# A retention and two-MoE kernel: the first stage reordered, with the weight conversion kept off GpSimd

## The chip, the cores and the metric

The kernel runs on one core of one Trainium2 chip. Its engines are called here as the profile calls them: PE (TensorE, matmuls), DVE (VectorE), ACT (ScalarE), POOL (GpSimd), SP (SyncE, which issues the DMAs). The metric is the device time of one execution in microseconds (us), the median of several runs; lower is better.

## The reference

Three operations follow each other on 3072 tokens (4 batches of 768) with 512 features:

```python
# retention: 8 heads of 64, a decaying state per head
for t in range(S):
    state = gamma[None, :, None, None] * state + np.einsum('bhd,bhe->bhde', k[:, :, t], v[:, :, t])
    y[:, :, t] = scale * np.einsum('bhd,bhde->bhe', q[:, :, t], state)
x = y.transpose(0, 2, 1, 3).reshape(3072, 512)
# first MoE, in fact one dense MLP; w_in is 512x2048, w_out 2048x512
r = np.maximum(x @ w_in, 0.0)
x = (s * (r * r) + b) @ w_out
# second MoE: 8 experts, each token goes to one of them by its sorted gate logits, 384 tokens per expert
logits = x @ w_gate
...
out[mask] = np.maximum(x[mask] @ w1[e], 0.0) @ w2[e]
```

The assignment of tokens follows the order of the logits, so the logits have to be nearly exact, and the kernel works with pairs of numbers: each operand of a large matmul is split into a high part in the type fp32r and the remainder, and three matmuls (high by high, high by low, low by high) stand for one.

## The kernel before, in words

The work is cut into 12 blocks of 256 tokens (0 to 11). Three blocks are one batch, and the retention state runs through them. A block goes through retention, `attn(blk, ...)`, which is four groups (two chunks of 128 tokens, two pairs of heads each), and then through the first MoE, which has 16 slices f of 128 hidden features.

A retention group has two parts. `b_part` issues 8 score matmuls (L330) and 4 mask multiplications on DVE into `am` (L334). `c_part` issues the state update (L347), the products of `am` with v (L353) and those of the state with q (L357), then the copy of the result to `xh` on ACT (L366) and the remainder `xl` on DVE (L367), and after every second group two state scalings on DVE (L373). `scale_chunk` multiplies the next chunk's q and v by decays on POOL (L197, L199). With `wide` the next group's `b_part` stands ahead of this group's `c_part`, with more banks and buffers; without it the parts alternate.

An MoE slice is an H unit and an X unit. `h_unit(blk, f, ...)` issues 12 matmuls of 256 columns (L417), ACT takes the relu into `r` (L420), DVE squares it by a product with the bank (L421); then `r_split` makes the high part `rh` on ACT (L425) and the remainder `rl` on POOL (L426). `x_unit(blk, f, ...)` issues 6 matmuls of 512 columns (L437) that need this pair. After slice 15 `x_out` copies two banks to SBUF on ACT (L447).

The 32 weight tiles (weight 2f is slice f of w_in, weight 2f+1 that of w_out) come as 64-bit words and are converted by `conv_gen`. Per weight: a square on ACT (L235), five operations on DVE (L258, L262, L265, L271, L275), then the high part on ACT (L245) and, on POOL, a subtraction (L247) and an addition (L249), after which the weight is in `READY`. Weights 20 to 31 use the memory of the first six chunks of q, k and v.

The logits of a chunk are eight products with a sum each on DVE (`gate`, L460, one for each expert). `logits_gen` waits for a chunk's result and meanwhile works on rows that depend on weights alone (`const_row`).

The order in which instructions are issued is written out at build time; nothing is moved afterwards. A `Side` is a generator that yields planned nanoseconds, a `Weave` issues units of PE work of planned cost and steps each side whose planned time has come. Each engine then runs its own queue in that order and waits by semaphores. In the first stage (lines 557 to 581):

- retention of blocks 0, 1 and 2 (wide), with conversion steps in between until weight 2 is ready;
- then `moe1((0, 1, 2), ...)`: for each f the H units of blocks 0, 1, 2, the X units two units behind; conversion goes on in between;
- after the last weight chunks 6 and 7 and the gate weights are loaded, and retention of block 3 (wide) runs alone;
- then the logits side is added, and the MoE of blocks 3, 4, ... follows, each woven with the next block's retention.

Of the kernel before, what the change touches and what calls it, by code (L numbers as in the profile page):

```python
# [20 lines left out]
F32 = mybir.dt.float32  # L21
# [60 lines left out]
def kernel(  # L82
# [16 lines left out]
    PRO=1.5,  # L99
    PN=2,  # L100
    CY=(560, 890),
# [4 lines left out]
    DV=(0, 2),  # L106
    WARM=24,
    XP=(1, 1),
# [120 lines left out]
    def conv_gen():  # L229
# [22 lines left out]
        for n in range(2 * NF):  # L252
# [13 lines left out]
            if last:  # L266
                parts(1)
            if n + 1 < 2 * NF:
                square(n + 1)
            yield CY[1]  # L270
            DVE.tensor_scalar(p.bitcast(I32), ai, -0x800000, None, op0=OP.bitwise_and)  # L271
            yield CY[0]
            if last:
                parts(2)
            DVE.scalar_tensor_tensor(p, lo32, 2.0 ** -52, p, op0=OP.mult, op1=OP.mult)  # L275
# [133 lines left out]
    def h_unit(blk, f, hb):  # L409
# [11 lines left out]
        DVE.scalar_tensor_tensor(r, ph, 0.0, r, op0=OP.max, op1=OP.mult)  # L421
# [41 lines left out]
    def logits_gen():  # L463


        for c in range(NC - 4):
# [51 lines left out]
    def conv_until(n):  # L518
        while n not in READY:
            conv.step()  # L520

    def moe1(blks, xbs, lag, apart=0):


        units = []
        seq = [(f, i) for f in range(NF - apart) for i in range(len(blks))]
        seq += [(f, i) for i in range(len(blks)) for f in range(NF - apart, NF)]
        for n in range(len(seq) + lag):
            if n < len(seq):
                def hu(n=n):  # L530
                    f, i = seq[n]
                    conv_until(2 * f + 1)
                    r = h_unit(blks[i], f, 2 + n % 2)
                    rhl = work.tile([128, 2, TB], F32R, name="rhl", bufs=3)
                    R2[blks[i], f] = r_split(r, rhl[:, 0], rhl[:, 1],
                                             DVE if len(blks) > 1 and n % DV[1] < DV[0] else POOL)
                units.append((1320, hu))
            if n >= lag:
                def xu(n=n - lag):
                    f, i = seq[n]  # L540
                    x_unit(blks[i], f, xbs[i])
                    if f == NF - 1:
                        x_out(blks[i])
                units.append((1300, xu))
        return units
# [11 lines left out]
    def attn3():  # L557
        for b in range(3):
            yield from attn(b, True)

    a3 = Side(attn3())
    conv.due = 3000.0
    while not a3.done:
        if conv.due < a3.due and PN not in READY:
            t = conv.due
            conv.step()
# [21 lines left out]
    for blk in range(3, NB - 2):  # L588
        nxt = Side(attn(blk + 1, False) if blk < NB - 3 else attn2())
        wv.add(nxt)  # L590
        units = moe1((blk,), ((0, 1),), 2)
# [549 lines left out]
```

## Time and profile before

| what | value |
|---|---|
| median of 3 runs | 1154.41 us (1153.56 to 1155.1) |
| profiled execution | 1160.23 us, span of its instructions 1158.5 us |
| PE busy, share of the span | 1044.8 us, 90% |
| DVE busy | 788.0 us, 68% |
| POOL busy | 581.7 us, 50% |
| ACT busy | 349.2 us, 30% |

The profiled execution is 5.8 us above the median; all sums below are made within the profiled execution. The trace gives the times of its instructions from the start of the span. The landmarks of the first stage are: first conversion instruction at 11.5 us, end of the retention of blocks 0 to 2 at 50.8 us, last weight ready at 219.9 us, retention of block 3 from 232.9 us, first MoE matmul of block 3 at 243.9 us.

### The profile page before, as it was taken

The page shows a single profiled execution, that of the slowest core. Times are in us where ns is not written, and L with a number is a line of the kernel's source. Part 1 is how long each engine was busy: PE and PEld are TensorE (multiplying, and loading weights), DVE is VectorE, ACT ScalarE, POOL GpSimd, SP SyncE. Part 2 cuts the span into 40 slices and gives each one's busy share as a digit, 9 for nine tenths or more (in the row PEclk, how much of TensorE's full clock was granted, in tenths as well). Part 3 has the DMA queues.
Part 4 walks back from the last instruction along what each step waited for, and adds up shares of the span by engine and source line. Part 5 has one row for each costly group of instructions (what it writes and reads, how often), then busy time and mean ns, then how long its engine had stood idle before and what let it go on. Part 6 is the DMA issues. An engine that isn't in the chain of part 4 may idle for free. (4 is left out here: it accounts for less than half of the span.)

```text
span 1158.5 us, 19641 instructions
## 1 busy us (share of the span) xinstructions
PE 1044.8 (90%) x7526; PEld 889.8 (77%) x7526; DVE 788.0 (68%) x1889; ACT 349.2 (30%) x776; POOL 581.7 (50%) x543
## 2 busy tenths in 40 slices
PE   6888777899999999999999999958988978989997
PEld 5766666788887878887888898747877767778996
DVE  5899999579979988979855533556667576572210
ACT  1333333322322222222222342123233333335511
POOL 4377777642355545464523342045354664648811
PEclk8999999999999999999999999978989989899999
DMA  9223222232120202021111000243243343426400
GB/s 322 90 91 91 92 91 91 71 103 74 55 82 20 73 10 71 23 81 36 58 46 47 25 1 1 81 130 119 84 137 119 119 133 106 145 81 201 137 28 28
DMA packets 31727, 98.29 MB, mean 85 GB/s; under 512 B 4496, under 2 KB 4880, under 8 KB 31632
## 3 DMA queue, kind: packets, MB, share of 16 engines
q1 hardware_dynamic: 27216, 83.40, 22.9%
q0 software_dynamic: 3840, 12.59, 3.2%
q8 instruction: 59, 0.97, 0.3%
q10 hardware_dynamic: 576, 1.05, 0.2%
q14 instruction: 36, 0.29, 0.1%
HBM read 84.43 MB, written 12.58 MB: 84 GB/s over the span
## 5 line engine op out<-in xcount | busy, mean ns | idle before, releaser
L460 DVE SCALAR_TENSOR_TENSOR scr<-tmp,wg 128x512 bf16<-128x512 f32 x288 | 260.5, 904 | 27.6 <-POOL tmp L485 22.4
L426 POOL TENSOR_TENSOR rhl<-r,rhl 128x256 fp32r<-128x256 f32 x160 | 133.8, 836 | 278.9 <-ACT rhl L425 220.3
L437 PE MATMUL b<-h,rhl 128*128 128x512 f32 x640 | 229.9, 402 | 3.6 <-ACT rhl L425 2.1
L954 POOL TENSOR_TENSOR l<-eraw,h 128x512 fp32r<-128x512 f32 x128 | 161.2, 1288 | 140.2 <-ACT h L953 114.9
L417 PE MATMUL b<-xh,h 128*128 128x256 f32 x704 | 204.9, 291 | 28.3 <-DVE r L421 26.9
L417 PE MATMUL b<-xh,l 128*128 128x256 f32 x704 | 199.6, 283 | 0.0
L417 PE MATMUL b<-xl,h 128*128 128x256 f32 x704 | 199.5, 283 | 0.0
L417 PEld LDWEIGHTS b<-xh,h 128*128 128x128 f32 x704 | 134.8, 192 | 45.5 <-DVE r L421 36.9
L437 PEld LDWEIGHTS b<-h,rhl 128*128 128x128 f32 x640 | 121.4, 191 | 32.2 <-ACT rhl L425 4.5
L417 PEld LDWEIGHTS b<-xl,h 128*128 128x128 f32 x704 | 135.0, 192 | 3.7
L417 PEld LDWEIGHTS b<-xh,l 128*128 128x128 f32 x704 | 134.9, 192 | 0.1
L425 ACT ACTIVATE rhl<-r 128x256 fp32r<-128x256 f32 x160 | 66.9, 418 | 224.4 <-DVE r L421 224.4
L421 DVE SCALAR_TENSOR_TENSOR r<-b,r 128x256 f32<-128x256 f32 x192 | 80.5, 419 | 79.3 <-ACT r L420 78.4
L437 PE MATMUL b<-l,rhl 128*128 128x512 f32 x320 | 127.4, 398 | 0.0
L420 ACT ACTIVATE r<-b 128x256 f32<-128x256 f32 x192 | 72.8, 379 | 175.1 <-PE b L417 166.4
L980 PE MATMUL b<-gh,h 128*128 128x384 f32 x256 | 95.4, 373 | 5.3 <-DVE hl L989 5.3
L980 PE MATMUL b<-gl,h 128*128 128x384 f32 x256 | 89.1, 348 | 0.0
L980 PE MATMUL b<-gh,l 128*128 128x384 f32 x256 | 89.0, 348 | 0.0
L983 ACT ACTIVATE hh<-b 128x384 fp32r<-128x384 f32 x64 | 31.5, 492 | 169.0 <-PE b L980 143.4
L1003 PE MATMUL b<-h,hh 128*128 128x512 f32 x192 | 81.6, 425 | 0.0
L1003 PE MATMUL b<-h,hl 128*128 128x512 f32 x192 | 78.0, 406 | 3.9 <-DVE hl L989 3.9
L989 DVE SCALAR_TENSOR_TENSOR hl<-b,hh 128x384 fp32r<-128x384 f32 x64 | 35.3, 552 | 67.0 <-ACT hh L983 64.5
(184 smaller groups left out, 1975.8 us busy)
## 6 DMA issues: line engine op xcount, KB each, us to landing
eraw<-in_w_dram SPq DMA_DIRECT2D x64, 512.0 KB, 3.7
q<-in_qkv_dram SPq DMA_DIRECT2D x36, 512.0 KB, 4.6
raw<-in_w_dram SPq DMA_DIRECT2D x32, 512.0 KB, 3.6
first<-in_qkv_dram SPq DMA_DIRECT2D x24, 256.0 KB, 6.0
x2d<-tmp SPq DMA_DIRECT2D x20, 256.0 KB, 5.7
wg<-in_wgT_dram SPq DMA_DIRECT2D x4, 512.0 KB, 3.8
x2d<-tmp ACTq DMA_DIRECT2D x4, 256.0 KB, 3.7
xg<-x2d,idx POOLq DMA_INDIRECT x24
```

What stands on the lines that cost most here:

```text
L417: PE.matmul(ph, a[:, ks], b[:, kc, :], start=(n == 0), stop=(n == 3 * KC - 1))
L420: ACT.activation(r, ph, AF.Relu)
L421: DVE.scalar_tensor_tensor(r, ph, 0.0, r, op0=OP.max, op1=OP.mult)
L425: ACT.activation(rh, r, AF.Copy)
L426: eng.tensor_tensor(rl, r, rh.bitcast(F32), op=OP.subtract)
L437: PE.matmul(X2[blk][t], a[:, ts], b, start=(f == 0 and i == 0), stop=(f == NF - 1 and i == 2))
L460: DVE.scalar_tensor_tensor(scr, x, 1.0, WG[e], op0=OP.mult, op1=OP.mult, accum_out=of[:, e:e + 1])
L954: POOL.tensor_tensor(lo, raw[:, a, :], hi.bitcast(F32), op=OP.subtract)
L980: PE.matmul(PH[0], a[:, ks], b[:, kc, :], start=(kc == 0 and n == 0), stop=(kc == KC - 1 and n == 2))
L983: ACT.activation(hh, PH[0], AF.Relu)
L989: DVE.scalar_tensor_tensor(hl, ph, 0.0, hh.bitcast(F32), op0=OP.max, op1=OP.subtract)
L1003: PE.matmul(Y[i, t], a[:, ts], b, start=(f == 0 and j == 0), stop=(f == NF2 - 1 and j == 2))
```

## The change

The two POOL operations of the conversion (L247, L249) go to DVE. For blocks 0 to 2 the square of an H unit goes from DVE to ACT (a new `act` argument of `h_unit`) and the remainder of `r_split` from POOL to DVE. In those blocks POOL keeps only `scale_chunk`.

The order of the first stage is written anew. Retention of block 0 is woven with conversion alone. Then conversion and the retention of blocks 1 and 2 are two sides (the retention not wide, planned at 0.45 of its usual pace); as soon as the two weights of a slice are ready, the H unit of block 0 for it is issued, with its X unit. Once the retention of blocks 1 and 2 has been issued, those two blocks are served first, each time the one that has done fewer slices, and block 0 takes slices when neither of them has a weight. X units follow three H units behind, or at once if no H unit can be issued. Chunks 6 and 7 are loaded when the conversion has been issued to its end. When blocks 1 and 2 are finished, the retention of block 3 (not wide) and the logits are added as sides, so that products of the gate stand between the parts of that retention. The planned costs of conversion steps change from (560, 890) to (500, 800), with two more yields for each weight.

```diff
-    CY=(560, 890),
+    CY=(500, 800),
+    SPACE=0.45,
...
             elif step == 1:
-                POOL.tensor_tensor(a, a, W[n][0].bitcast(F32), op=OP.subtract)
+                DVE.tensor_tensor(a, a, W[n][0].bitcast(F32), op=OP.subtract)
             else:
-                POOL.tensor_tensor(W[n][1], a, p, op=OP.add)
+                DVE.tensor_tensor(W[n][1], a, p, op=OP.add)
                 READY.add(n)
...
-        DVE.scalar_tensor_tensor(r, ph, 0.0, r, op0=OP.max, op1=OP.mult)
+        if act:
+            ACT.activation(r, r, AF.Square)
+        else:
+            DVE.scalar_tensor_tensor(r, ph, 0.0, r, op0=OP.max, op1=OP.mult)
         return r
...
-        for c in range(NC - 4):
+        for c in (2, 3, 4, 5, 0, 1, *range(6, NC - 4)):
...
-    a3 = Side(attn3())
+    a0 = Side(attn(0, True))
     conv.due = 3000.0
-    while not a3.done:
-        if conv.due < a3.due and PN not in READY:
-            t = conv.due
-            conv.step()
-            conv.due = t + PRO * (conv.due - t)
+    while not a0.done:
+        min((conv, a0), key=lambda x: x.due).step()
+
+    def attn12():
+        for b in (1, 2):
+            yield from attn(b, False, SPACE)
+
+    a12 = Side(attn12(), a0.due)
+    wv = Weave([conv, a12])
...
+    def h_first(b, f, hb):
+        R2[b, f] = split_to_work(h_unit(b, f, hb, True), DVE)
+        pend.append((b, f))
...
+    while len(OUT) < 3:
+        if conv.done and CPB not in QKV:
+            load_chunk(CPB)
+            load_chunk(CPB + 1)
+            scale_chunk(CPB)
+        if a4 is None and {1, 2} <= OUT:
+            load_gate()
+            a4 = Side(attn(3, False, SPACE), wv.t)
+            wv.add(a4)
+            tail = Side(logits_gen(), wv.t)
+            wv.add(tail)
+        can = [b for b in ((1, 2) if a12.done else ()) + (0,) if at[b] < NF and 2 * at[b] + 1 in READY]
+        can = can[:1] if 0 in can[:1] else sorted((b for b in can if b), key=lambda b: at[b])
+        if len(pend) > 2 or (pend and not can):
+            wv.unit(1300, x_first)
+        elif can:
+            b = can[0]
+            wv.unit(1320, lambda: h_first(b, at[b], 2 + nh % 2))
+            at[b] += 1
+            nh += 1
         else:
-            a3.step()
-    conv.due = 0.0
-    wv = Weave([conv])
-    for u in moe1((0, 1, 2), ((4, 5), (6, 7), (0, 1)), 2):
-        wv.unit(*u)
-    conv_until(2 * NF - 1)
-    load_chunk(CPB)
-    load_chunk(CPB + 1)
-    scale_chunk(CPB)
-    load_gate()
-    a4 = Side(attn(3, True), wv.t)
-    wv.add(a4)
+            s = min((s for s in wv.sides if not s.done), key=lambda s: s.due)
+            wv.t = max(wv.t, s.due)
+            s.step()
     wv.until(lambda: a4.done)
-    tail = Side(logits_gen())
-    wv.add(tail)
```

Three places on DVE show what is moved. Line numbers of the changed kernel differ: L255, L259, L262, L269, L274 are its five conversion operations, L244 and L246 the two that came from POOL, L428 the remainder of an H unit, L423 the square of the later blocks, L333 `am`, L366 `xl`, L372 the state scaling, L462 the gate.

In the middle of the conversion the queue of before has the five operations of a weight, with the squares of H units (L421) among them:

```order
L258 TENSOR_SCALAR tmp<-raw 128x512
L262 SCALAR_TENSOR_TENSOR tmp<-raw,tmp 128x512
L265 SCALAR_TENSOR_TENSOR tmp<-tmp 128x512
L421 SCALAR_TENSOR_TENSOR r<-b_1856,r 128x256
L271 TENSOR_SCALAR tmp<-tmp 128x512
L275 SCALAR_TENSOR_TENSOR tmp<-raw,tmp 128x512
```

The changed kernel has seven there, and remainders (L428) among them:

```order
L255 TENSOR_SCALAR tmp<-raw 128x512
L259 SCALAR_TENSOR_TENSOR tmp<-raw,tmp 128x512
L428 TENSOR_TENSOR rhl<-r,rhl 128x256
L262 SCALAR_TENSOR_TENSOR tmp<-tmp 128x512
L244 TENSOR_TENSOR tmp<-tmp,h_1822 128x512
L269 TENSOR_SCALAR tmp<-tmp 128x512
L246 TENSOR_TENSOR l_1823<-tmp 128x512
L274 SCALAR_TENSOR_TENSOR tmp<-raw,tmp 128x512
```

Both subtractions and additions of a weight now share the queue with the operations on the next weight.

In the retention of block 1 the queue of before holds the `am` of two groups, one conversion step between them, and one more ahead of the first group's `xl`:

```order
L334 SCALAR_TENSOR_TENSOR am<-b_311,mask 128x128
L334 SCALAR_TENSOR_TENSOR am<-b_312,mask 128x128
L334 SCALAR_TENSOR_TENSOR am<-b_311,mask 128x128
L334 SCALAR_TENSOR_TENSOR am<-b_312,mask 128x128
L265 SCALAR_TENSOR_TENSOR tmp<-tmp 128x512
L334 SCALAR_TENSOR_TENSOR am<-b_326,mask 128x128
L334 SCALAR_TENSOR_TENSOR am<-b_327,mask 128x128
L334 SCALAR_TENSOR_TENSOR am<-b_326,mask 128x128
L334 SCALAR_TENSOR_TENSOR am<-b_327,mask 128x128
L271 TENSOR_SCALAR tmp<-tmp 128x512
L367 SCALAR_TENSOR_TENSOR xl<-b_339,xh 128x2x128
```

In the changed kernel the second group of block 1 has the first MoE unit between its two parts (PE runs scores, H unit of block 0, X unit of block 0, then the group's second part):

```order
L333 SCALAR_TENSOR_TENSOR am<-b_353,mask 128x128
L333 SCALAR_TENSOR_TENSOR am<-b_354,mask 128x128
L333 SCALAR_TENSOR_TENSOR am<-b_353,mask 128x128
L333 SCALAR_TENSOR_TENSOR am<-b_354,mask 128x128
L246 TENSOR_TENSOR l_331<-tmp 128x512
L428 TENSOR_TENSOR rhl<-r,rhl 128x256
L274 SCALAR_TENSOR_TENSOR tmp<-raw,tmp 128x512
L366 SCALAR_TENSOR_TENSOR xl<-b_396,xh 128x2x128
L372 TENSOR_TENSOR sbd<-b_195,sdec 64x4x64 x2
```

The remainder of that H unit stands ahead of the group's `xl`. This arrangement occurs in two of the eight groups of blocks 1 and 2.

In the retention of block 3 the queue of before holds nothing but that retention:

```order
L334 SCALAR_TENSOR_TENSOR am<-b_2217,mask 128x128
L334 SCALAR_TENSOR_TENSOR am<-b_2218,mask 128x128
L334 SCALAR_TENSOR_TENSOR am<-b_2217,mask 128x128
L334 SCALAR_TENSOR_TENSOR am<-b_2218,mask 128x128
L367 SCALAR_TENSOR_TENSOR xl<-b_2229,xh 128x2x128
L373 TENSOR_TENSOR sbd<-b_2182,sdec 64x4x64 x2
```

In the changed kernel gate products stand between its parts:

```order
L333 SCALAR_TENSOR_TENSOR am<-b_2216,mask 128x128
L333 SCALAR_TENSOR_TENSOR am<-b_2217,mask 128x128
L333 SCALAR_TENSOR_TENSOR am<-b_2216,mask 128x128
L333 SCALAR_TENSOR_TENSOR am<-b_2217,mask 128x128
L462 SCALAR_TENSOR_TENSOR scr,L<-tmp,wg 128x512 x2
L366 SCALAR_TENSOR_TENSOR xl<-b_2232,xh 128x2x128
L372 TENSOR_TENSOR sbd<-b_2172,sdec 64x4x64 x2
L462 SCALAR_TENSOR_TENSOR scr,L<-tmp,wg 128x512 x2
```

Sixteen of them stand ahead of that block's last `xl`.

## Rows read from the trace of the kernel before

**Rows 1.** Windows: PE, PEld, DVE, ACT, POOL busy (x instructions), clock, DMA share, GB/s

```profile
11.00:50.00 39.00, 31.25 (x244) 24.73 (x244) 31.79 (x81) 8.39 (x20) 20.34 (x16) 0.82 0.68 240
60.00:216.00 156.00, 120.29 (x709) 99.50 (x709) 151.60 (x173) 56.85 (x132) 121.61 (x94) 0.99 0.29 91
...
233.00:244.00 11.00, 9.56 (x97) 7.54 (x97) 5.95 (x23) 2.25 (x6) 4.85 (x5) 1.00 0.35 103
244.00:600.00 356.00, 347.20 (x2369) 300.68 (x2370) 305.46 (x770) 94.65 (x239) 167.04 (x158) 0.99 0.17 51
```

**Rows 2.** Waits of PE from 11 to 244 us: total, times, longest

```profile
PE b L417 <- DVE r L421: 35.7, 30, 2.5
```

**Rows 3.** Timeline of DVE: start, duration, line, operation, tiles

```profile
109.85 0.42 DVE L421 SCALAR_TENSOR_TENSOR r<-b,r 128x256 f32<-128x256 f32 x1
110.18 0.68 DVE L275 SCALAR_TENSOR_TENSOR tmp<-raw,tmp 128x512 f32<-128x512 uint32 x1
110.78 0.42 DVE L258 TENSOR_SCALAR tmp<-raw 128x512 int32<-128x512 int32 x1
111.23 1.11 DVE L262 SCALAR_TENSOR_TENSOR tmp<-raw,tmp 128x512 int32<-128x512 int32 x1
...
204.41 1.66 DVE L262 SCALAR_TENSOR_TENSOR tmp<-raw,tmp 128x512 int32<-128x512 int32 x1
```

**Rows 4.** Timeline of POOL around the same moments, idle time before in brackets

```profile
107.19 1.73 POOL L247 TENSOR_TENSOR tmp<-tmp,h 128x512 f32<-128x512 f32 x1
110.79 1.00 POOL L426 TENSOR_TENSOR rhl<-r,rhl 128x256 fp32r<-128x256 f32 x1 [1.88 <-ACT rhl L425]
...
204.05 1.48 POOL L249 TENSOR_TENSOR l<-tmp 128x512 fp32r<-128x512 f32 x1
```

**Rows 5.** Timeline of DVE, a product of two SBUF tiles of 512 columns

```profile
6.28 0.69 DVE L197 TENSOR_TENSOR first<-first,qdec 128x512 f32<-128x512 f32 x1
```

**Rows 6.** Timeline of DVE, L258 of weights 0, 4, 8 and 31

```profile
11.52 1.37 DVE L258 TENSOR_SCALAR tmp<-raw 128x512 int32<-128x512 int32 x1
...
50.71 0.42 DVE L258 TENSOR_SCALAR tmp<-raw 128x512 int32<-128x512 int32 x1
...
75.69 1.52 DVE L258 TENSOR_SCALAR tmp<-raw 128x512 int32<-128x512 int32 x1
...
209.92 1.17 DVE L258 TENSOR_SCALAR tmp<-raw 128x512 int32<-128x512 int32 x1
```

**Rows 7.** Timeline of PE, first matmul of an H, its X and the next H

```profile
224.44 0.28 PE L417 MATMUL b<-xh,h 128*128 128x256 f32 x1
...
225.88 0.40 PE L437 MATMUL b<-h,rhl 128*128 128x512 f32 x1
...
227.26 0.28 PE L417 MATMUL b<-xhs,h 128*128 128x256 f32 x1
```

**Rows 8.** Timeline of ACT, relu and high part of H units

```profile
111.14 0.36 ACT L420 ACTIVATE r<-b 128x256 f32<-128x256 f32 x1
112.71 0.42 ACT L425 ACTIVATE rhl<-r 128x256 fp32r<-128x256 f32 x1 [1.21 <-DVE r L421]
```

**Rows 9.** Timeline, one retention group: its `am` on DVE, its copy on ACT

```profile
41.67 0.89 DVE L334 SCALAR_TENSOR_TENSOR am<-b,mask 128x128 f32<-128x128 f32 x4
...
43.72 0.38 ACT L366 ACTIVATE xhs<-b 128x256 fp32r<-128x256 f32 x1 [3.16 <-PE b L357]
```

**Rows 10.** Timeline, end of the stage: last weight (POOL), retention and MoE of block 3 (PE)

```profile
218.58 1.29 POOL L249 TENSOR_TENSOR l<-tmp 128x512 fp32r<-128x512 f32 x1
232.89 1.58 PE L330 MATMUL b<-q 64*128 64x128 f32 x16
243.90 0.39 PE L417 MATMUL b<-xh,h 128*128 128x256 f32 x1 [0.29 <-DVE xl L367]
```

**Rows 11.** Timeline of DVE, a gate product with POOL idle

```profile
249.34 0.68 DVE L460 SCALAR_TENSOR_TENSOR scr<-tmp,wg 128x512 bf16<-128x512 f32 x1
...
250.06 1.17 DVE L460 SCALAR_TENSOR_TENSOR scr<-tmp,wg 128x512 bf16<-128x512 f32 x1
```

More of the change, by code (lines that the diff above doesn't have):

```diff
@@ L105 @@
     FZ=(8390, 160),
-    DV=(0, 2),
     WARM=24,
-    XP=(1, 1),
     AG=2,
@@ L265, in conv_gen @@
             DVE.scalar_tensor_tensor(a, p, TINY_WORD * TINY_WORD, a, op0=OP.is_ge, op1=OP.mult)
-            if last:
-                parts(1)
             if n + 1 < 2 * NF:
@@ L270, in conv_gen @@
             yield CY[1]
+            if last:
+                parts(1)
+                yield CY[1]
             DVE.tensor_scalar(p.bitcast(I32), ai, -0x800000, None, op0=OP.bitwise_and)
@@ L274, in conv_gen @@
                 parts(2)
+                yield CY[1]
             DVE.scalar_tensor_tensor(p, lo32, 2.0 ** -52, p, op0=OP.mult, op1=OP.mult)
@@ L407, in split_last, with h_unit @@
             DVE.tensor_tensor(xl[:, ps], XF[i], xh[:, ps].bitcast(F32), op=OP.subtract)
-    def h_unit(blk, f, hb):
+    def h_unit(blk, f, hb, act=False):
         xh, xl = XT[blk]
@@ L516, in const_end, with split_to_work, moe1, hu @@
         ACT.activation(csum[:, 0:E], pc[:, 0:E], AF.Copy)
-    def conv_until(n):
-        while n not in READY:
-            conv.step()
-    def moe1(blks, xbs, lag, apart=0):
+    def split_to_work(r, eng):
+        rhl = work.tile([128, 2, TB], F32R, name="rhl", bufs=3)
+        return r_split(r, rhl[:, 0], rhl[:, 1], eng)
+    def moe1(blk, xb, lag):
         units = []
[L526 to L536, printed above, removed]
+        for n in range(NF + lag):
+            if n < NF:
+                def hu(f=n):
+                    R2[blk, f] = split_to_work(h_unit(blk, f, 2 + f % 2), POOL)
                 units.append((1320, hu))
             if n >= lag:
-                def xu(n=n - lag):
-                    f, i = seq[n]
-                    x_unit(blks[i], f, xbs[i])
+                def xu(f=n - lag):
+                    x_unit(blk, f, xb)
                     if f == NF - 1:
-                        x_out(blks[i])
+                        x_out(blk)
                 units.append((1300, xu))
@@ L555 @@
     scale_chunk(0, DVE)
-    def attn3():
-        for b in range(3):
-            yield from attn(b, True)
-    a3 = Side(attn3())
+    a0 = Side(attn(0, True))
     conv.due = 3000.0
-    while not a3.done:
-        if conv.due < a3.due and PN not in READY:
-            t = conv.due
-            conv.step()
-            conv.due = t + PRO * (conv.due - t)
-        else:
-            a3.step()
-    conv.due = 0.0
-    wv = Weave([conv])
-    for u in moe1((0, 1, 2), ((4, 5), (6, 7), (0, 1)), 2):
-        wv.unit(*u)
@@ L574 @@
-    conv_until(2 * NF - 1)
-    load_chunk(CPB)
-    load_chunk(CPB + 1)
-    scale_chunk(CPB)
-    load_gate()
-    a4 = Side(attn(3, True), wv.t)
-    wv.add(a4)
+    while not a0.done:
[5 more added lines that the diff above has]
+    wv = Weave([conv, a12])
+    wv.t = a0.due
+    XBS = {0: (0, 1), 1: (4, 5), 2: (6, 7)}
+    at = {0: 0, 1: 0, 2: 0}
+    pend = []
@@ new lines, with x_first @@
+    a4 = None
+    nh = 0
+    def h_first(b, f, hb):
+        R2[b, f] = split_to_work(h_unit(b, f, hb, True), DVE)
+        pend.append((b, f))
+    def x_first():
+        b, f = pend.pop(0)
+        x_unit(b, f, XBS[b])
+        if f == NF - 1:
+            x_out(b)
+            OUT.add(b)
+    OUT = set()
+    while len(OUT) < 3:
[18 more added lines that the diff above has]
+            nh += 1
+        else:
+            s = min((s for s in wv.sides if not s.done), key=lambda s: s.due)
+            wv.t = max(wv.t, s.due)
+            s.step()
@@ L590 @@
         wv.add(nxt)
-        units = moe1((blk,), ((0, 1),), 2)
+        units = moe1(blk, (0, 1), 2)
         for i, u in enumerate(units):
```

2 lines of the change are left out of this document (removed).

## The prediction, made before the changed kernel ran

> **What bounds the kernel now.** I read the windows first, because the kernel has stages with different limits. From 244 to 600 us (MoE of the later blocks) PE is busy 347.2 of 356 us [rows 1]: PE is the limit there and 8.8 us are idle. From 60 to 216 us, the conversion of the weights with the MoE of blocks 0 to 2, PE is busy 120.3 of 156 us, DVE 151.6 (97%) and POOL 121.6 [rows 1]: DVE is the limit. The waits of PE agree: 35.7 us of its idle time up to 244 us end with the square on DVE that an H unit needs [rows 2]. So I looked at what occupies DVE. L258 of weight 8 starts at 75.69 and that of weight 31 at 209.92 [rows 6]: 134.2 / 23 = 5.84 us for a weight. A conversion operation on 512 columns takes 0.68 us (L275) or 0.42 (L258), and the same kind of operation also 1.11 or 1.66 us [rows 3]. The difference is POOL: at 110.2 us, where L275 takes 0.68, POOL has ended its L247 at 108.9 and starts again at 110.79; the L262 of 204.41, with 1.66, lies beside the L249 of 204.05 [rows 4]. L421, which reads a PSUM bank, has 0.42 even so. After the last weight (219.9) PE has 13 us of MoE left; at 232.9 the retention of block 3 starts, alone, and the first H unit of block 3 at 243.9 [rows 10]. In those 11 us DVE and PE pass work to and fro (6.0 and 9.6 us busy [rows 1]).
>
> **The change, part by part.** The first stage ends for this sum where H of block 3 starts, 243.9 us now.
>
> 1. Conversion on DVE with POOL idle. The starts in [rows 3] are 0.33 us apart behind L421 (duration 0.42), 0.60 behind L275 (0.68), 0.45 behind L258, whose result the next one needs. So a three-operand operation costs 0.60 to 0.71 and a two-operand one 0.34 to 0.45. The two operations from POOL are of the kind of L197, 0.69 us for 512 columns [rows 5], 0.61 in a chain; this price rests on one row, and its bounds are 0.42 and 0.71. A weight is then 0.45 + 0.71 + 0.60 + 0.61 + 0.34 + 0.61 + 0.60 = 3.9 us (3.5 to 4.3) against 5.84 now. The remainder of an H unit, 256 columns, has no row; half of L197 and L421 bound it at 0.35 and 0.42, in a chain 0.34.
>
> 2. Retention of blocks 0 to 2. Now this and the conversion of weights 0 to 3 take from 11.52 to 50.71 us [rows 6], 39.2 us. Up to the start of weight 8 the changed order has on DVE four weights more (15.6), the two moved operations of the first four (4 x 1.22 = 4.9) and three remainders (1.0). The conversion beside POOL goes: three weights' pairs on POOL of some 1.5 us each stretch DVE now by about half their time, -4 (0 to -7; POOL keeps the scaling of the chunks). Six groups without `wide` wait some 0.5 us for `xl`, since the chain from the end of `am` (42.56) to the end of the copy (44.10) is 1.54 us [rows 9] and some 1.1 us of conversion stand in between: +3. In two groups an H and an X unit stand between the scores and the second part. An H unit is 1.44 us on PE and an X unit 1.38 [rows 7]; relu and high part on ACT are 0.36 and 0.42 [rows 8], the square, which ACT does not do on such a tile now, lies between those, 1.3 us together with the hand-overs. So `xl` comes 1.44 + 1.3 + 0.4 + 1.38 + 0.6 (state update) + 1.54 = 6.7 us after the scores, while DVE has 2.5 us of work: 4.2 us idle, twice, and 1 us at the third early unit, +9.4. Sum: 39.2 + 21.5 - 4 + 3 + 9.4 = 69.1; weight 8 starts at 80.6, and I take 82 because the clock of these 39 us is 0.82 and not 1 [rows 1]. Bounds: 78 (half of the waits) and 93 (PE at 1.2 GHz throughout, below). That is later than now (75.7): this step loses 6 us.
>
> 3. MoE of blocks 0 to 2 from there. PE has 45 H and 44 X units until retention of block 3: 45 x 1.44 + 44 x 1.38 = 125.5 us. DVE has 24 weights x 3.9 + 45 remainders x 0.34 = 109 us. So the limit changes from DVE to PE. DVE queues the remainders among the conversion steps and may have to wait for PE there, and PE for DVE elsewhere; I take 3 us for that (0 to 10), since blocks 1, 2 and 0 alternate and X units come three units behind. PE ends the second part of block 2's last group 1.5 us before weight 8, so the MoE units end at 80.5 + 125.5 + 3 = 209, against 232.9 now.
>
> 4. Retention of block 3. Now 11.0 us. Sixteen gate products come into its DVE queue; a product takes 0.72 us from start to start with POOL idle [rows 11]. Those between `am` and `xl` are hidden by the 1.54 us chain; eight others are not: 5.8 us. One X unit of block 0 adds 1.4. The scaling of chunks on POOL beside gate products (1.17 instead of 0.68 [rows 11]) and the groups without `wide` add some 3. Sum 21 us (17 to 27): H of block 3 starts at 230, 13.9 us earlier than now. So the retention of block 3 isn't hidden; the gate work takes its cover away.
>
> 5. Behind it. The sixteen products are not to be done later, and DVE, busy 305 of 356 us there, holds PE a little less. All PE could gain is its 8.8 us of idle time [rows 1]; most PE time there passes without a wait, so I take 1.5 (0 to 5). The loads: chunks 6 and 7 are issued behind the last weight's load and arrive during the MoE units; the gate weights wait for two staging tiles that are freed with the last weight, beside 4 us of MoE work. If that cover fails, the first gate products hold `xl` of block 3 by 2 to 3 us. The search and the experts behind are not touched. I cost ACT at nothing: a square more for each of 48 units is 0.4 us beside 2.8 us of PE for that unit.
>
> Sum in the profiled execution: 1160.2 - 13.9 - 1.5 = 1144.8 us. That execution is 5.8 us above the median of the runs, so the median of the changed kernel comes to 1139 us.
>
> **A rule weighed against it.** In the retention PE has less to do for a microsecond than now, since the same groups are spread over 70 us with three MoE units. The granted clock of that stretch is 0.82 now, and 0.99 in the MoE behind it [rows 1], so part of it already runs at 1.2 GHz of 2.4. The Trainium skill, "TensorE: Matmul & The Clock Gate", section "What's actually happening", has the throttled state as the default, released by activity; the two windows agree. By that rule the retention could stay at the lower level to its end; what this costs is rival B.
>
> **The rivals.**
> A. Everything fits: DVE does not wait in the retention (weight 8 at 78), no loss between DVE and PE, block 3's retention in 17 us, 4 us gained behind. 76.5 + 125.5 + 17 = 219, so 24.9 + 4 = 29 us less: 1125. For it: conversion operations do take 0.68 and 0.42 without POOL. Against it: the waits for PE that the new order puts into DVE's queue.
> B. PE runs at 1.2 GHz through the retention. Then H, X and second part double in the two groups with MoE units (+4.3 each) and the six others wait some 0.5 us more: weight 8 at about 93, H of block 3 at 91.5 + 125.5 + 3 + 21 = 241, 4.4 us gained in all: 1150. For it speaks 0.82; against it that PE was at full clock in the MoE with 77% busy.
> C. The other side: DVE and PE go in lockstep through the remainders. Up to weight 20 DVE has 12 weights (46.8 us) and 24 remainders; if each of these finds the ACT chain just begun, it waits 1.3 us with all conversion behind it: 46.8 + 24 x 1.64 = 86 instead of PE's 63.5 + 3. That is 20 us more: H of block 3 at 250, 6 us later than now, nothing gained behind: 1160. It decides from a wait of 1.1 us for each remainder, where the 15.4 us are used up. For it: in the changed queue the remainder follows the H unit's place directly. Against it: two banks and two `r` buffers let PE begin the next H units before DVE arrives.
> D. The change doesn't do what it says: DVE's long operations are not due to POOL. Then a weight is 5.2 us for its five operations and 1.7 for two more; from a weight 8 at about 88, 24 x 6.9 + 15 = 181 us on DVE lead to 269, and H of block 3 starts at 290, 46 us later than now: 1200. Rows 3 and 4 speak against it.
>
> **How the numbers follow.** Forecast 0.45, A 0.27, B 0.15, C 0.10, D 0.03. About 2.3 us (0.2%) either way can't be told from no change. Faster by more than that: all of the forecast and A and most of B (0.12): 0.84; within it: the rest of B and a little of C: 0.05; slower: C and D: 0.11. The forecast's own bounds, with the terms of steps 2 to 4 at 4 us either side, are 1131 to 1147. The range goes from 1121 (A with the moved operations at their lower bound) to 1156, past B: it leaves out C, D and the edge of A.
>
> **What would show it.** Conversion operations at 0.68 and 0.42 us through the first 200 us (step 1). The eighth weight's L255 near 82 us, idle DVE time ended by ACT's `xh` and by the high part in the retention (step 2). PE nearly without waits from there to the retention of block 3 at about 209 (step 3), that retention 21 us long with gate products in DVE's queue (step 4), and behind it the same durations as now. The prediction is wrong if the granted clock stays at half through the MoE, if remainders (L428) wait over 1.1 us each on ACT, or if DVE's operations stay above 1 us without POOL.

## The result, and the profile after

The changed kernel takes 1141.46 us (median of four runs, 1141.29 to 1144.58) where the kernel before takes 1154.76 beside it: a ratio of 0.9889 [0.9865, 0.9912], 13.3 us less. The forecast was 1139. Its profiled execution takes 1141.49 us with a span of 1139.7. The profiled execution of before lay 5.8 us above its median, so the two spans differ by 18.8 us. 15.75 of these are there when H of block 3 starts. Of the other 3.0, 0.5 is there by the last H matmul of the first MoE, which starts 16.3 us earlier (706.2 before, 689.9 now). The medians differ by 2.4 us less than the traces' first stages do, so nothing behind the first stage is counted as an effect here.

The windows of the changed kernel, columns as in [rows 1]:

```profile
11.00:50.00 39.00, 26.21 (x179) 20.96 (x180) 32.40 (x68) 9.05 (x20) 13.79 (x10) 0.82 0.65 239
50.00:77.00 27.00, 19.59 (x129) 15.26 (x129) 20.64 (x51) 8.22 (x19) 0.00 (x0) 0.88 0.18 59
77.00:194.00 117.00, 114.89 (x733) 103.75 (x732) 105.47 (x199) 75.18 (x169) 5.73 (x4) 1.00 0.34 104
208.00:228.00 20.00, 14.31 (x102) 11.22 (x102) 16.66 (x53) 3.69 (x8) 3.02 (x2) 0.83 0.23 68
228.00:584.00 356.00, 346.58 (x2381) 300.31 (x2380) 295.61 (x748) 95.68 (x239) 166.30 (x158) 1.00 0.16 51
```

Read them against [rows 1]. In the MoE of blocks 0 to 2 (third line) PE is now busy 114.9 of 117 us, where it was 120.3 of 156, and POOL has almost nothing to do. The limit there is PE. Before that stage stand 66 us (first two lines) in which PE is busy for 45.8 us and DVE for 53: neither is full, and each has waits that the other or ACT ends (step 2 below). Behind it stand 20 us of retention of block 3, where it was 11. So the middle is tight and both ends have room.

The timeline of PE shows the landmarks that answer to [rows 10]: the MoE units in an unbroken row from 75.28, the retention of block 3 at 208.30 (before: 232.89), H of block 3 at 228.15 (before: 243.90).

```profile
75.28 0.56 PE L416 MATMUL b<-xh,h 128*128 128x256 f32 x1
75.64 0.41 PE L416 MATMUL b<-xl,h 128*128 128x256 f32 x1
...
77.24 0.28 PE L416 MATMUL b<-xh,h 128*128 128x256 f32 x1
...
208.30 1.24 PE L329 MATMUL b<-q 64*128 64x128 f32 x8 [0.41 <-issue]
...
228.15 0.39 PE L416 MATMUL b<-xh,h 128*128 128x256 f32 x1
```

### The profile page after: what moved, and what is told of

Its sections match the earlier page's. It is cut to its first block, busy times and chain, and to the rows that moved or that the text cites. A ratio compares the mean times of both kernels' runs of the same rounds, so it can differ in the third digit from the quotient of the medians.

```text
span 1139.7 us, 19546 instructions
## 1 busy us (share of the span) xinstructions
PE 1045.2 (92%) x7526; PEld 896.5 (79%) x7526; DVE 760.9 (67%) x1953; ACT 374.7 (33%) x824; POOL 440.5 (39%) x431
## 5 line engine op out<-in xcount | busy, mean ns | idle before, releaser
L462 DVE SCALAR_TENSOR_TENSOR scr<-tmp,wg 128x512 bf16<-128x512 f32 x288 | 258.7, 898 | 30.3 <-POOL tmp L487 21.8
L439 PE MATMUL b<-h,rhl 128*128 128x512 f32 x640 | 227.2, 402 | 7.6 <-ACT rhl L427 6.4
L428 POOL TENSOR_TENSOR rhl<-r,rhl 128x256 fp32r<-128x256 f32 x112 | 88.2, 788 | 230.9 <-ACT rhl L427 172.2
L423 DVE SCALAR_TENSOR_TENSOR r<-b,r 128x256 f32<-128x256 f32 x144 | 60.5, 420 | 75.4 <-ACT r L419 74.7
L194 POOL TENSOR_TENSOR q<-q,qdec 128x512 f32<-128x512 f32 x18 | 29.3, 1629 | 169.3 <-DMA q<-in_qkv_dram 169.2
```

Of the source, the lines that this page charges most:

```text
L194: eng.tensor_tensor(qT, qT, qdec, op=OP.mult)
L428: eng.tensor_tensor(rl, r, rh.bitcast(F32), op=OP.subtract)
L439: PE.matmul(X2[blk][t], a[:, ts], b, start=(f == 0 and i == 0), stop=(f == NF - 1 and i == 2))
L462: DVE.scalar_tensor_tensor(scr, x, 1.0, WG[e], op0=OP.mult, op1=OP.mult, accum_out=of[:, e:e + 1])
```

## The experiments

Two theories were to be told apart. By the prediction's, the gain is a balance: the freed DVE and the early units win more than the spread retention and the gate products in block 3's retention lose. By its rival, the moves of work between engines do it all, and the new order adds little or costs. In the table, "MoE" is the first H unit of an unbroken row, "block 3" the start of its retention on PE, "H" the first H matmul of block 3; ratios are to the kernel before, measured beside each kernel. Where a median and a ratio of two rows disagree, the ratio is the one to compare, since the kernel before takes 1151.42 to 1156.53 us beside them.

| kernel | MoE | block 3 | H | median, us | ratio |
|---|---|---|---|---|---|
| changed | 75.3 | 208.3 | 228.2 | 1141.46 | 0.9889 [0.9865, 0.9912] |
| changed, conversion back on POOL | 75.5 | 218.2 | 239.4 | 1150.65 | 0.9991 [0.9974, 1.0009] |
| engine moves alone | 52.2 | 195.5 | 206.5 | 1116.28 | 0.9700 [0.9672, 0.9727] |
| changed, wide retention | 53.1 | 195.5 | 216.7 | 1132.97 | 0.9773 [0.9744, 0.9802] |
| changed, gate later | 77.5 | 208.6 | 221.7 | 1134.73 | 0.9849 [0.9815, 0.9883] |
| changed, measured again | 78.7 | 211.4 | 232.6 | 1147.02 | 0.9909 [0.9876, 0.9942] |
| changed, no early units | 71.8 | 211.4 | 232.5 | 1147.17 | 0.9918 [0.9892, 0.9944] |
| old order, conversion on DVE only | 50.1 | 211.2 | 222.2 | 1140.06 | 0.9877 [0.9842, 0.9912] |
| old order, remainder and square only | 48.7 | 218.1 | 229.0 | 1144.15 | 0.9894 [0.9868, 0.9921] |
| engine moves alone, again | 49.5 | 192.8 | 203.8 | 1120.81 | 0.9695 [0.967, 0.972] |

**The conversion back on POOL.** The changed kernel with the two conversion operations back on POOL; the square stays on ACT and the remainder on DVE:

```diff
-                DVE.tensor_tensor(a, a, W[n][0].bitcast(F32), op=OP.subtract)
+                POOL.tensor_tensor(a, a, W[n][0].bitcast(F32), op=OP.subtract)
...
-                DVE.tensor_tensor(W[n][1], a, p, op=OP.add)
+                POOL.tensor_tensor(W[n][1], a, p, op=OP.add)
```

> The changed kernel with the subtraction and the addition of the conversion put back on POOL (the new order, the square on ACT and the remainder on DVE stay). Theory T (the time comes from taking POOL off the two-input operations beside DVE): the five DVE operations of a weight rise again from 0.42 and 0.69 us to a mean of about 1.0 us, the conversion runs at 5.5 to 6 us a weight, DVE is the limit again, and the MoE of blocks 0 to 2 ends at about 225 to 235 us instead of 208; median 1158 to 1170. Rival O (the time comes from the order, that block 0's MoE starts with the first weights): no more than 5 us above the changed kernel, at most 1146.

Measured: 1150.65 against 1151.42, no difference from the kernel before that can be measured, and between the two ranges: both missed. In its instruction groups on DVE from 80 to 180 us (line, operation, tiles, count | busy, mean ns | idle before) the long operations are back:

```profile
L255 DVE TENSOR_SCALAR tmp<-raw 128x512 int32<-128x512 int32 x18 | 26.2, 1458 | 0.0
L428 DVE TENSOR_TENSOR rhl<-r,rhl 128x256 fp32r<-128x256 f32 x33 | 23.6, 717 | 0.7 <-ACT rhl L427 0.7
```

L255 has 1458 ns on average beside POOL and 420 in the changed kernel. A weight takes (206.91 - 77.20) / 23 = 5.64 us, as Theory T had it. The retention of block 3 starts at 218.2, not at 225 to 235.

This is not the order without any engine move: the square and the remainder are still moved, and no run has the order alone. What it has to be set against is the old order with just those two moved (1144.15 in the table, described below). PE's rows, first of this run, then of that one:

```profile
218.18 1.24 PE L329 MATMUL b<-q 64*128 64x128 f32 x8 [0.41 <-issue]
239.36 0.58 PE L416 MATMUL b<-xh,h 128*128 128x256 f32 x1
```

```profile
218.07 1.56 PE L330 MATMUL b<-q 64*128 64x128 f32 x16
229.04 0.39 PE L417 MATMUL b<-xh,h 128*128 128x256 f32 x1 [0.29 <-DVE xl L367]
```

So the 14.7 us by which the retention of block 3 comes earlier than before (232.9) belong to the moves; the order brings nothing forward here and takes 21.2 us for that retention instead of 11.0. Its price is 0.0097 of the ratio, 11 us, with intervals that do not touch.

**The engine moves alone.** The kernel before with the two operations and all remainders of the three-block MoE on DVE, and that MoE's squares on ACT:

```diff
-    DV=(0, 2),
+    DV=(2, 2),
...
-                POOL.tensor_tensor(a, a, W[n][0].bitcast(F32), op=OP.subtract)
+                DVE.tensor_tensor(a, a, W[n][0].bitcast(F32), op=OP.subtract)
...
-                POOL.tensor_tensor(W[n][1], a, p, op=OP.add)
+                DVE.tensor_tensor(W[n][1], a, p, op=OP.add)
...
-                    r = h_unit(blks[i], f, 2 + n % 2)
+                    r = h_unit(blks[i], f, 2 + n % 2, len(blks) > 1)
```

> The kernel before in its own order (wide retention of blocks 0 to 2, then the three blocks slice by slice, retention of block 3 alone) with the engine moves alone: subtraction and addition of the conversion on DVE, square of blocks 0 to 2 on ACT, their remainder on DVE. Theory T: the weights come at about 4.3 us (28 weights x 3.9 + 48 remainders x 0.34 = 126 us on DVE from 50 us on), PE needs 135 us from 51 us on, so the MoE of blocks 0 to 2 ends at 187 to 200 us instead of 232.9 and the first H unit of block 3 starts at about 205, which is earlier than the 228 of the changed kernel; median 1115 to 1127, faster than the changed kernel. Rival O: without the new order less than 5 us below the kernel before, 1150 to 1155.

Measured: 1116.28 us, 35.1 less than before and more than twice the gain of the changed kernel. Its PE timeline:

```profile
52.24 0.39 PE L417 MATMUL b<-xh,h 128*128 128x256 f32 x1 [0.93 <-DVE xls L367]
...
195.54 1.56 PE L330 MATMUL b<-q 64*128 64x128 f32 x16
206.52 0.39 PE L417 MATMUL b<-xh,h 128*128 128x256 f32 x1 [0.29 <-DVE xl L367]
```

This settles the main question: without the new order the moves gain more. Against these rows the changed kernel starts its unbroken MoE 23.0 us later (75.28), needs 10.3 us less for it (133.0 instead of 143.3, since three early H units and their X units are done and one X unit is left for block 3's retention), and 8.9 us more for the retention of block 3 (19.85 instead of 10.98): 21.6 us, the difference of the two starts of H. The medians, each against the kernel before beside it, are 35.1 - 13.3 = 21.8 us apart; measured again, the two ratios (0.9695 and 0.9909) differ by some 25 us.

**The old wide retention in the changed kernel.** This and the next two split the order's price.

```diff
-    def attn12():
-        for b in (1, 2):
-            yield from attn(b, False, SPACE)
+    def attn3():
+        for b in range(3):
+            yield from attn(b, True)
...
-        can = [b for b in ((1, 2) if a12.done else ()) + (0,) if at[b] < NF and 2 * at[b] + 1 in READY]
+        can = [b for b in (1, 2, 0) if at[b] < NF and 2 * at[b] + 1 in READY]
```

> The changed kernel with one part of its order undone: the retention of blocks 0 to 2 as before (wide, all three ahead of the MoE, conversion until weight 2 in between); the rest stays (engine moves, service of blocks 1, 2 and 0, the retention of block 3 with gate products). Theory T (the new order loses PE time between 11 and 76 us, where weight 8 comes at 77 with 3 slices done, while e2 has started its three blocks at 52): the MoE of blocks 0 to 2 ends at 194 to 202 us instead of 208, H of block 3 starts at 213 to 222; 8 to 15 us below the changed kernel and 5 to 11 us above e2. Rival (the gate products in the retention of block 3 are the whole loss against e2): within 3 us of the changed kernel.

Measured: 1132.97 us, in its range against the changed kernel (0.9773 against 0.9889 and 0.9909) and 12.2 us above the engine moves alone beside it (1120.81), 1.2 more than expected. Its PE timeline:

```profile
53.13 0.39 PE L416 MATMUL b<-xh,h 128*128 128x256 f32 x1 [0.93 <-DVE xls L366]
...
195.51 0.34 PE L329 MATMUL b<-q 64*128 64x128 f32 x1 [0.41 <-issue]
...
216.70 0.58 PE L416 MATMUL b<-xh,h 128*128 128x256 f32 x1
```

The retention of block 3 starts at 195.5, as with the engine moves alone, and 13 to 16 us before the changed kernel's (208.3, 211.4). That is the price of the spread retention, early units included (they alone make no difference, below). What is left to the 206.5 of the engine moves alone is block 3's retention, 21.2 us instead of 11.0.

**The gate later.** The changed kernel with the gate's products joined after block 3's retention:

```diff
-            tail = Side(logits_gen(), wv.t)
-            wv.add(tail)
...
+    tail = Side(logits_gen())
+    wv.add(tail)
```

> The changed kernel with the logits added as a side only after the retention of block 3 (as before), so that no gate product stands in DVE's queue there. Theory T: that retention shrinks from 20 us (208.3 to 228.2) to 12 to 14 us, since eight exposed products of 0.72 us and their hand-overs go; the gate work is done later under PE's cover, where at most 2 us are lost; median 1134 to 1138, 4 to 8 us below the changed kernel. Rival G (the gate work done there is missed later, PE waits for DVE): no difference beyond 1.5 us, 1140 to 1143.

Measured: 1134.73 us, 0.9849, some 0.4% below the changed kernel's ratio, with intervals that overlap slightly. The trace is clearer:

```profile
208.55 1.24 PE L329 MATMUL b<-q 64*128 64x128 f32 x8 [0.41 <-issue]
...
221.69 0.39 PE L416 MATMUL b<-xh,h 128*128 128x256 f32 x1
```

The retention takes 13.1 us instead of 19.8, from the same start. So between these two traces 6.7 of the 8.9 us are the gate's products, and 2.1 are left to the narrow groups and the X unit in it. The other traces with the gate in that retention have 21.2 to 22.3 us for it.

**No early units of block 0.**

```diff
-        can = [b for b in ((1, 2) if a12.done else ()) + (0,) if at[b] < NF and 2 * at[b] + 1 in READY]
+        can = [b for b in ((1, 2, 0) if a12.done else ()) if at[b] < NF and 2 * at[b] + 1 in READY]
```

> The changed kernel without MoE units before the retention of blocks 1 and 2 is issued: block 0 starts with blocks 1 and 2. Theory T: the three early slices save PE 3 x 2.82 = 8.5 us later, but each stands in the way of the retention (DVE idle 1 to 3 us before xl), so weight 8 comes at 68 to 72 us instead of 77 and the time is within 3 us of the changed kernel (e8), either way. Rival O (the early start of block 0 is what the change gains by): 6 us or more above e8.

> The changed kernel once more, unaltered, so that the others of this call and the kernel before can be set against it on one chip: 10 to 16 us below the kernel before.

Measured beside each other: 1147.17 us without the early units and 1147.02 for the changed kernel as it is, 0.9918 and 0.9909. The early units gain nothing that can be measured: weight 8 comes at 73.6 without them (68 to 72 expected) and at 80.4 with them, and the units left over take up the difference (block 3 at 211.4 in both). The changed kernel's second measurement, 9.5 us below the before, is just short of what was expected; its interval overlaps the first one's.

**One move at a time.** The kernel before with only the two conversion operations on DVE, and with only the remainders on DVE and the squares on ACT:

> The kernel before in its own order, with one engine move alone: the subtraction and the addition of the conversion on DVE; the square stays on DVE and the remainder on POOL. Theory T (two-input operations on POOL stretch those on DVE): POOL keeps 48 remainders of some 0.75 us, 36 us of work instead of 134, so most of the stretch goes, but not all; the MoE of blocks 0 to 2 ends at 205 to 218 us and the time lies between e2 and the kernel before, nearer to e2: 14 to 24 us below the kernel before. If the remainder alone mattered (rival): less than 5 us below it.

> The kernel before in its own order, with the other engine moves alone: square of blocks 0 to 2 on ACT and their remainder on DVE; subtraction and addition of the conversion stay on POOL. Theory T: POOL still runs 32 x 2 operations of 1.3 to 1.7 us beside DVE, whose conversion operations keep a mean above 0.95 us, and the remainder, with two SBUF inputs, is stretched too; 0 to 6 us below the kernel before. Rival: half of the gain of e2 or more (over 17 us below).

Measured: 1140.06 and 1144.15 us against 1156.53, 16.5 and 12.4 less. The first lies in its range; the second is far above its 0 to 6, and both theories missed. The timeline of DVE in the second, and POOL's of the same microseconds below it, tell why:

```profile
121.26 1.52 DVE L258 TENSOR_SCALAR tmp<-raw 128x512 int32<-128x512 int32 x1
122.70 1.50 DVE L429 TENSOR_TENSOR rhl<-r,rhl 128x256 fp32r<-128x256 f32 x1
124.12 0.68 DVE L262 SCALAR_TENSOR_TENSOR tmp<-raw,tmp 128x512 int32<-128x512 int32 x1
124.83 0.69 DVE L265 SCALAR_TENSOR_TENSOR tmp<-tmp 128x512 f32<-128x512 f32 x1
...
120.76 1.74 POOL L247 TENSOR_TENSOR tmp<-tmp,h 128x512 f32<-128x512 f32 x1 [2.09 <-DVE tmp L271]
122.57 1.34 POOL L249 TENSOR_TENSOR l<-tmp 128x512 fp32r<-128x512 f32 x1
```

L258 and L429 start while POOL works and end 0.28 and 0.29 us behind POOL's ends (122.50, 123.91); L262 and L265, with POOL idle, are short. In the kernel before POOL had the remainders too: from 80 to 180 us it was busy 78.6 of the 100 us and not 54.5, and the five operations of a weight took 5.33 us together on average and not 4.42 (L265: 1.28 and 0.69). So an operation that leaves POOL can give DVE back up to 1.1 us. I had priced the move by the work that it puts on DVE, and not by the stretching that leaves with it. The square left DVE in the same run, 0.41 us for each unit, and the 35.7 us of PE's waits that it ended [rows 2] gave way to 21.4 us that end with the remainder. How the 12.4 us divide between the remainder and the square no run shows. Together the moves gain 35 us, 6 more than their sum (28.9).

**The last scaling of the chunks.** In the changed kernel DVE's operations grow long once more near the end of the MoE, with POOL's scaling beside them. The first run put that scaling later in program order:

```diff
             load_chunk(CPB)
             load_chunk(CPB + 1)
+        if a4 is None and {1, 2} <= OUT:
             scale_chunk(CPB)
-        if a4 is None and {1, 2} <= OUT:
             load_gate()
```

> The changed kernel with the scaling of chunk 6 on POOL issued only when the MoE of blocks 1 and 2 is finished, instead of beside the last weights. Theory T: the scaling beside the last weights stretched L259, L262 and L269 of weights 30 and 31 (1.55, 1.60, 1.26 us), made PE wait 2 us for a weight and dropped its clock for 5 us; without it the MoE of blocks 0 to 2 ends 3 to 6 us earlier (202 to 205), but the retention of block 3 waits 1 to 2.5 us for its chunk: median 1137 to 1141. Rival: the wait for the chunk takes all of it back or more, 1141 to 1145.

Measured: 1139.85 us, 0.9896, the changed kernel's ratio. But the edit did not act. POOL's timeline of this run:

```profile
195.22 1.49 POOL L196 TENSOR_TENSOR q<-q,vdec 128x512 f32<-128x512 f32 x1 [8.06 <-DMA q<-in_qkv_dram]
```

POOL waits 8 us for the load and starts at once when it is there: nothing else stands in its queue, so the place in the program delays nothing. The run says nothing on the theory. The next one uses data: a copy of one column of the last weight, on POOL, ahead of the scaling, in the kernel with the engine moves alone, beside that kernel once more.

```diff
+    POOL.tensor_copy(csum[:, 0:1], W[2 * NF - 1][1][:, 0:1].bitcast(F32))
     scale_chunk(CPB)
```

> e2 (order of before, engine moves) with the scaling of chunks 6 and 7 on POOL held back, by a copy of one column that reads the last weight, until the conversion is finished. Theory T: the four POOL operations of 5.6 us no longer stretch L258, L262 and L271 of the weights near the end; the conversion ends 2 to 4 us earlier and POOL does its work beside PE's last 12 us of MoE: 0 to 4 us below e2. Rival: PE has enough work ahead, no difference beyond 1 us.

> e2 once more, unaltered, as the reference of e9, e10 and e11 on one chip: 0.967 to 0.973 of the kernel before.

```profile
177.89 0.32 POOL L580 COPY csum<-l 128x1 f32<-128x1 f32 x1 [145.98 <-DVE l L249]
```

Now it acts. In the window from 150 to 180 us (columns as above) PE gains, first with the copy, then without:

```profile
150.00:180.00 30.00, 29.91 (x187) 25.58 (x187) 28.58 (x57) 19.19 (x44) 2.11 (x3) 1.00 0.38 123
```

```profile
150.00:180.00 30.00, 26.62 (x162) 22.25 (x161) 29.66 (x51) 16.52 (x38) 5.92 (x4) 1.00 0.32 104
```

PE is busy 3.3 us more, and from weight 8 to the end of the MoE 118.6 us pass instead of 122.3. Medians: 1116.11 and 1120.81 against 1155.88, 0.9657 [0.9635, 0.9678] and 0.9695 [0.967, 0.972]; the intervals overlap by 0.0008, so in the total time the 4.7 us, just above the 0 to 4 expected, are likely, not shown. The first of the two is the best version of all: 39.8 us below the kernel before, where the change as it is gained 13.3.

**More conversion during the wide retention**, in the kernel with the engine moves alone:

```diff
-    PRO=1.5,
-    PN=2,
+    PRO=1.0,
+    PN=4,
```

> e2 with more conversion woven into the retention of blocks 0 to 2 (until weight 4 is ready instead of 2, planned at its own pace and not at 1.5 of it). Theory T: DVE is busy 32 of 39 us in the retention of e2 and is the limit of the whole stage (99% busy from 80 to 180 us), so idle DVE time used there comes off the end: 0 to 5 us below e2. Rival: each conversion step there stands in the way of am or xl, the retention takes as much longer: 0 to 6 us above e2.

Measured: 1128.95 us, 8 slower than without it (1120.81), more than the 0 to 6 of the rival. The first unit of the MoE comes at 61.0 us instead of at 49.5 to 52. A wait of PE from 11 to 62 us (total, times, longest), and the window from 11 to 61 us:

```profile
PE b L353 <- DVE am L334: 4.4, 2, 3.2
```

```profile
11.00:61.00 50.00, 33.15 (x245) 25.96 (x245) 42.65 (x101) 11.28 (x23) 12.50 (x10) 0.79 0.59 206
```

Without the extra conversion that wait is 0.6 us (11 to 50) and the granted clock 0.95 (11 to 49.5). So what the conversion puts into DVE's queue delays `am`, and PE with it; how much of the 11.5 us the wait makes up, and how much the clock, is not shown. Nothing comes back for it: by 62 us DVE has done L265 for six weights in either kernel, and the MoE of blocks 0 to 2 takes 144.1 us here and 143.3 without. It resembles the changed order's loss: conversion that is spread into the retention keeps PE from the whole MoE that stands before it.

## Why the prediction was right

The total was right: H of block 3 was put at 230 and comes at 228.15 in the profiled execution; the forecast of 1139 is 2.5 us off, inside its own range of 1131 to 1147. The ratio measured again, 0.9909, would put it at 1144. The mechanism was right too: DVE's operations are short without POOL, the limit moves to PE, and both retentions get longer. That the sum comes so near is in part luck. Step 2 ends 5.2 us too late, with larger errors inside it that offset each other, step 3 is 4.5 us too short, step 4 1.2 too long: 1.9 us remain.

**Step 1, the price of the conversion: right.** The timeline of DVE in the MoE of the changed kernel answers to [rows 3]:

```profile
99.71 0.69 DVE L259 SCALAR_TENSOR_TENSOR tmp<-raw,tmp 128x512 int32<-128x512 int32 x1
...
101.05 0.68 DVE L244 TENSOR_TENSOR tmp<-tmp,h 128x512 f32<-128x512 f32 x1
101.74 0.43 DVE L428 TENSOR_TENSOR rhl<-r,rhl 128x256 fp32r<-128x256 f32 x1
102.08 0.42 DVE L269 TENSOR_SCALAR tmp<-tmp 128x512 int32<-128x512 int32 x1
102.41 0.69 DVE L246 TENSOR_TENSOR l<-tmp 128x512 fp32r<-128x512 f32 x1
...
103.62 0.42 DVE L255 TENSOR_SCALAR tmp<-raw 128x512 int32<-128x512 int32 x1
```

The moved operations (L244, L246) take 0.68 to 0.69 us, and the remainder, which had only bounds, 0.43. L255 follows L255 at 5.18 us on average (77.03 to 196.11 for 23 weights), more than the 3.9 of work: some 1.8 remainders for each weight stand between, and DVE is idle 11.5 of the 117 us (third window above), 0.5 us a weight, which end mostly with the high part on ACT. Rival D is refuted: the same operations grow long when POOL gets the two back and are short when it doesn't.

**Step 2, the retention: near in its sum, by errors that offset each other.** Weight 8 starts at 77.03, not 82. DVE's waits in the retention of the changed kernel, 11 to 80 us:

```profile
DVE xl L366 <- ACT xh L365: 7.1, 6, 2.8
DVE xls L366 <- ACT xhs L365: 5.0, 4, 2.0
```

That is 12.1 us, close to the 12.4 that were put in. But those were added to the 39.2 us of before, which hold such waits already (kernel before, 11.52 to 50.71 us):

```profile
DVE xl L367 <- ACT xh L366: 6.5, 6, 2.0
DVE xls L367 <- ACT xhs L366: 1.2, 2, 0.9
```

So the order added 4.4 us of waits where 12.4 were put in: the two groups with units between the scores and the second part have 2.77 and 1.99 us instead of 4.2 each. DVE's own work (third busy time) grew by more than was put in. The windows up to weight 8, first after, then before:

```profile
10.95:77.03 66.08, 45.83 (x306) 36.26 (x307) 53.12 (x120) 17.35 (x38) 13.84 (x10) 0.85 0.46 165
```

```profile
11.52:50.71 39.19, 31.25 (x244) 24.73 (x244) 31.79 (x83) 8.58 (x20) 20.17 (x16) 0.83 0.66 234
```

That is 21.3 us more, where 21.5 - 4 = 17.5 were put in. The stretching that was to go stayed: before, L258 and L262 were 4.9 us longer there than alone; now POOL's scaling of the chunks, which remains, holds seven conversion operations for 5.7 us in all. The 1.4 us that were put on for the clock were not needed.

**Step 3, PE as the limit: right; the coupling was 7.5 us and not 3.** The units take 133.0 us from 75.28 on, to 208.30, where 125.5 + 3 were put in. Waits of PE from 77 to 209 us:

```profile
PE b L439 <- DVE l L246: 2.5, 2, 2.0
PE b L329 <- issue: 0.4, 1, 0.4
PE b L416 <- DVE l L246: 0.3, 1, 0.3
```

The longest is near the end, at 194.96, where POOL scales the last chunk. DVE there, and POOL below it:

```profile
189.26 1.55 DVE L259 SCALAR_TENSOR_TENSOR tmp<-raw,tmp 128x512 int32<-128x512 int32 x1
...
189.22 1.04 POOL L196 TENSOR_TENSOR q<-q,vdec 128x512 f32<-128x512 f32 x1 [8.64 <-DVE tmp L255]
```

Then the clock is 0.66 for five microseconds:

```profile
195.00:200.00 5.00, 5.00 (x15) 3.85 (x16) 4.96 (x11) 1.85 (x4) 0.00 (x0) 0.66 0.32 108
```

The waits (2.8), the issue (0.4), these five microseconds (0.34 x 5 = 1.7) and the first H at half clock (0.8: its matmuls last 0.41 us until 76.9, then 0.28) make 5.7 of the 7.5 us; the rest no row here explains. That the scaling is behind the waits was shown only in the old order, where holding it back gave PE 3.3 us. Rival C, the lockstep, needed 1.1 us of wait for each remainder; L428 waits 9.6 us in 19 events from 77 to 205 us, the longest 0.9, in a DVE that has time for it. It is refuted.

**Step 4, retention of block 3: right.** 19.85 us, 21 predicted. The products stand in DVE's queue ahead of `am`:

```profile
213.00 0.68 DVE L462 SCALAR_TENSOR_TENSOR scr<-tmp,wg 128x512 bf16<-128x512 f32 x1
...
215.07 0.88 DVE L333 SCALAR_TENSOR_TENSOR am<-b,mask 128x128 f32<-128x128 f32 x4
```

PE waits 3.9 us for `am` there. The run with the gate later puts the products at 6.7 us; 5.8 were worked out. What is left, 2.1 us, was put at 1.4 + 3.

**Step 5, behind it: too large.** 9.4 of 356 us of PE are idle (last line of the windows) where 8.8 were. Of the 1.5 us of relief 0.5 is there at the last H matmul.

**Rival A** had the limits right and the waits at nothing. Its 78 for weight 8 is nearer to 77.03 than the forecast's 82, but the waits of step 2 are there, and so are 7.5 us of coupling where it had none and 19.85 us for block 3's retention where it had 17. **Rival B**, half clock through the retention: the granted clock is 0.82 and 0.88 in its two windows, so only a part of it ran at 1.2 GHz, and the level rose with the first units in a row (0.41 us to 0.28 at 76.9). The Trainium skill, "TensorE: Matmul & The Clock Gate", section "What's actually happening", has the throttled state as the default and activity as what releases it; these rows agree. In the second measurement the clock was 0.72 from 11 to 50 us and H of block 3 came at 232.6, about a third of the way from 228.2 to B's 241; 1.3 us of that is a longer retention of block 3.

**What the prediction did not ask.** It had the two losses of the order among its terms, 6 us in step 2 and 10 in step 4, and summed them with the gain of step 3 as one change. It never asked what the engine moves give in the old order. Its own numbers would have told: from the end of the old retention at 50.8 us, 48 H and X units at 1.44 + 1.38 are 135.4 us, with 3 of coupling and the old 11.0 for block 3 H comes at 200, 44 us earlier. Measured were 206.5 and 35 us in the total.

## What to carry to other kernels

Where a change moves work between engines and also reorders it, work out each part without the other: here the engine moves are the whole gain, and the order that came with them takes back 22 of 35 us (11 us where the conversion was still the limit). When a stage turns from one engine's limit to another's, ask when that other engine can start its long unbroken row of work, and keep short latency-bound stages whole in front of it rather than spread among preparations. The price of an operation on POOL includes what it holds up on DVE; when work leaves POOL, count that too.

## What the hardware showed that I had not expected

- The same spread retention came out at different lengths with its clock. At a granted clock of 0.85, 0.78, 0.75 and 0.71 from 11 to 80 us, weight 8 started at 77.0, 79.2, 80.4 and 82.6 us (changed kernel, gate later, changed again, scaling later; the code up to there is the same). It can't be told from this which is cause and which effect.
- POOL does not slow DVE's operations down, it holds them. Of the 47 DVE operations of the kernel before that read SBUF alone and start from 100 to 180 us while a POOL operation is under way, 46 end at a fixed distance behind POOL's end: L258 and L271 (0.42 us alone) 0.27 to 0.29 us, L262, L265 and L275 (0.69) 0.53 to 0.56, which is their own duration less 0.14 us, however long POOL had left. The 47th began in the same 0.01 us as POOL and took 0.41 us. One that began before POOL is not touched: L258 at 110.78 [rows 3], with POOL from 110.79 [rows 4]. L421, which reads PSUM, runs at 0.41 to 0.42 beside POOL. So what POOL costs is the rest of its own operation less 0.14 us, and the shorter the DVE operation, the worse the ratio. The Trainium skill, "SBUF — State Buffer", section "SBUF: two separate sides", calls the shared port pair of the two engines an exclusive lock: the one that starts first holds it for its whole instruction and the other fully blocks. For DVE it names operations with two SBUF inputs, against a POOL operation that reads SBUF, and those in a 2-port mode. These distances agree; L262, L265 and L275 have two SBUF inputs, L421 has one, and which mode L258 and L271 ran in no row shows. The gain of the engine moves could be estimated operation by operation from these distances; that was not done here.
